# Attention and two MoE layers on one core: K and Q of the second pair loaded earlier, a third V buffer, block sums copied by DMA, a shorter warm-up

## The chip, the core and the metric

The kernel runs on one core of one Trainium2 chip. The time is that of one execution on the device in microseconds (us), and the median over three runs is what counts. The engines of the core are TensorE (PE; its weight loads are shown apart as PEld), VectorE (DVE), ScalarE (ACT), GpSimd (POOL) and SyncE (SP), whose queue issues most of the DMAs. Each engine takes its own list of instructions in order and waits on semaphores.

## What is computed

```
block, window = 32, 16            # q, k, v: (2, 8, 768, 64); nb = 24 blocks
k_sum = max of k over each block; v_sum = mean of v over each block
s_l = scale * q k^T, kept only where |i - j| < window
s_s = scale * q k_sum^T + log(block)
a = softmax over [s_l, s_s];  x = a @ [v, v_sum]
u = x + (relu(x^T w_tok1) w_tok2)^T         # tokens
y = u + relu(u w_ch1) w_ch2                 # channels, 1536 wide
out = y + relu(norm(y) * g w2_ch1) w2_ch2   # channels, 2048 wide
```

## The kernel before

**Attention.** Two heads make a pair; there are eight pairs. A pair has three quads of four windows of 64 queries, so 24 quads run in all. A window of 64 queries sees 96 keys and 24 block entries, so every score row has 120 columns. For a quad n the steps are: `att_qk` (PE, tile `scores`), `att_exp` (the mask step on DVE into `sn` with its minimum `mn`, then the exponential on ACT into `pr`), `att_tr` (PE transposes into `pt`), `att_evac` (copy of `pt` to `PT`, on DVE for every third quad, else on ACT), `att_av` (PE, `av`), `att_norm` (DVE: reciprocal `rec`, product into `u`), `att_hi` (ACT: `xh`) and `att_lo` (POOL: `xl`).

**Preparation of a pair i.** `load_pair` loads K and Q, `load_vt` the transposed V, `load_v` the two halves of V (rows for even and odd windows). `prep_k` takes block maxima of K on DVE (`ks`), and `copy_k` writes them in seven copies into K on ACT. `prep_v1` sums VT over blocks: for pair 0 in one DVE reduction, for the others in four halving steps and two last sums on POOL, into `Z`. `prep_v2` transposes `Z` on PE (`psv`) and copies the result, scaled by 1/32, into 24 rows of V for each of six windows: four ACT instructions for two halves and two heads. So V's rows are 96 rows of values, 24 of block sums, and one guard row that a DMA fills once. Column 64 of the block rows is one; it was set by a memset. K, Q have three buffers, V, VT and Z two.

**Weights.** `load_half` loads 512 KB of weights into a `stage` buffer (three of them). A tick of `conversion` takes the absolute value on ACT (`dec`, L114), four DVE operations (L128 to L136), a rounded copy on ACT (`wh`, L176) and the rest on DVE (`wl`, L183). In attention two such operations go with each `att_norm`. The MoE matmuls (`g1`, `g2`, then `g3`, `g4`) use the high and low parts. Parts of `g1` and `g2` are woven into attention.

**Order.** `ORDER` gives each step a position in units of a quad; `attention` sorts all steps by position and emits them. A builder then makes a fixed list for every engine from that, in which an instruction whose inputs it takes to come late can stand behind later ones: in the trace POOL's list has `xl` of quad 0 (position 6.25) ahead of the sums of pair 1 (position 0.3). The list does not change at run time. The score tile has two slots in shared banks, so the scores of a quad wait for the mask step of the quad before.

**Start.** The first loads stand in `run`: K(0), mask, ident, VT(0), V(0), guard rows, K(1), Q(1), g, VT(1), V(1), all on SP; only Q(0) is on ACT's queue. 24 warm-up matmuls, in blocks of six fp32r and bf16 ones by turns, stand ahead of the first scores in PE's list.

Of the kernel before, what the change touches and what calls it, by code (L numbers as in the profile page):

```python
# [10 lines left out]
F32 = mybir.dt.float32  # L11
F32R = mybir.dt.float32r
U32 = mybir.dt.uint32
AF = mybir.ActivationFunctionType
# [4 lines left out]
P = 128  # L19
B, H, S, D = 2, 8, 768, 64  # L20
BLOCK, WINDOW = 32, 16
NB = S // BLOCK
# [4 lines left out]
NK = 96 + NB  # L27
VC = 136
# [3 lines left out]
LEAD = 3  # L32
NXN = 3
ORDER = {
    "load_k": -5.2, "load_vt": -6.45, "load_v": -0.2, "kmax": -1.75, "copy_k": -0.45, "vsum": -2.7,
    "vput": -0.15, "vput0": 1.35, "kmax1": -2.05, "copy1": -1.35, "vsum0": -3.0, "exp": 1.0, "tr": 2.1,
    "evac": 3.15, "av": 3.65, "norm": 4.55, "hi": 4.85, "lo": 6.25, "late": 22.53, "conv": 4.0, "ops": 2,
    "bg": 9, "bgd": 1.04, "bgt": 0.05, "fin": 0.16,
# [11 lines left out]
def f32(ap):  # L50
    return ap.bitcast(F32)


class Kern:
# [161 lines left out]
    def load_v(self, i):  # L216
        nc = self.nc
        b, p = divmod(i, NPAIR)
        V = self.V[i % 2]
        nc.sync.dma_start(V[NB:NK, 0], self.v[b, p, 0])  # L220
        nc.sync.dma_start(V[0:96, 1], self.v[b, p, 1])

# [34 lines left out]

    def prep_v2(self, i):
        nc = self.nc
        V, Z = self.V[i % 2], self.Z[i % 2]  # L260
        ps = self.ps_pt.tile([P, 512], F32, tag="pt", name=f"psv{i}")
        nc.tensor.transpose(ps[:NK, 0:P], Z, self.ident)  # L262
        for a, j in ((0, 0), (96, 1)):
            for r in range(2):
                nc.scalar.activation(  # L265
                    V[a : a + NB, j, :, 65 * r : 65 * r + 64],
                    ps[a : a + NB, r * 64 : r * 64 + 64]
                    .rearrange("p (o n) -> p o n", o=1)
                    .to_broadcast([NB, 6, 64]),
                    AF.Copy,  # L270
                    scale=1.0 / BLOCK,
                )

    def att_qk(self, n):
        nc = self.nc
# [58 lines left out]
    def att_av(self, n):  # L334
        nc = self.nc
        i, qd = divmod(n, 3)
        V = self.V[i % 2]
        pt = self.pt.pop(n)
        ps = self.ps_av.tile([P, 2, 132], F32, tag="av", name=f"av{n}")
        self.av[n] = ps  # L340
        for e in range(2):
            for r in range(2):
                for j in range(2):
                    u = 2 * e + j
                    nc.tensor.matmul(  # L345
                        ps[64 * j : 64 * j + 64, e, 65 * r : 65 * r + 65],
                        pt[:, u * P + 64 * (r ^ j) : u * P + 64 * (r ^ j) + 64],
                        V[:, j, 2 * qd + e, 64 * r : 64 * r + 65],
                        start=True,
                        stop=True,  # L350
                    )
# [264 lines left out]
    def run(self):  # L616
        tc, nc, ctx = self.tc, self.nc, self.ctx
# [26 lines left out]
        att = self.att  # L644
        self.Q = [att.tile([P, S], F32, name=f"Q{i}") for i in range(3)]
        self.K = [att.tile([P, 7, 184], F32, name=f"K{i}") for i in range(3)]
        self.PT = [att.tile([NK + 1, 512], F32, name=f"PT{i}") for i in range(2)]
        self.V = [att.tile([NK + 1, 2, 6, VC], F32, name=f"V{i}") for i in range(2)]
        self.VT = [att.tile([P, S], F32, name=f"VT{i}") for i in range(2)]
        self.Z = [att.tile([P, NK], F32, name=f"Z{i}") for i in range(2)]  # L650
        self.u = const.tile([P, B * ST, C], F32, name="u")
# [5 lines left out]
        self.hh = [xp.tile([P, 2, C], F32R, name=f"hh{i}") for i in range(B)]  # L657
        self.hl = [xp.tile([P, 2, C], F32R, name=f"hl{i}") for i in range(B)]

        warm = [att.tile([P, 512], dt, name=f"warm{i}") for i, dt in enumerate((F32R, mybir.dt.bfloat16))]  # L660
        nc.vector.memset(f32(warm[0]), 0.0)
        nc.gpsimd.memset(warm[1], 0.0)
        for t in self.Z:
            nc.gpsimd.memset(t, 0.0)
        for t in self.V:
            nc.gpsimd.memset(t[0:NB, 0, :, 64:65], 1.0)
            nc.gpsimd.memset(t[96:NK, 1, :, 64:65], 1.0)
        for t in self.PT:
            nc.vector.memset(t[96 : NK + 1], 1.0)
        self.load_pair(0, nc.scalar)  # L670
        nc.sync.dma_start(self.mask, self.mask_in)
        nc.sync.dma_start(self.ident, self.ident_in)
        self.load_vt(0)
        self.load_v(0)
        for t in self.V:
            nc.sync.dma_start(t[NK : NK + 1], self.guard)
        self.load_pair(1)
        nc.sync.dma_start(self.gt, self.g)
        self.load_vt(1)
        self.load_v(1)  # L680

        wps = self.ps_mm.tile([P, 512], F32, tag="mm", name="warm_ps")
        for i in range(24):
            w = warm[i // 6 % 2]
            nc.tensor.matmul(wps, w[:, :P], w, start=True, stop=True)  # L685

        self.attention()
        actx.close()
# [27 lines left out]
        for n in range(len(units) + 1):  # L716
# [3 lines left out]
            if n < len(units):  # L720
                kind, s, f, g = units[n]
                nf = F1 if kind == "u" else F2
                c = 3 + f if kind == "u" else 3 + F1 + f
# [117 lines left out]
```

## Time and profile before

| | |
|---|---|
| median of 3 runs | 604.87 us (603.02 to 605.31) |
| profiled execution, its own time | 604.47 us |
| its span, first to last instruction | 602.7 us |
| mean granted TensorE clock | 0.977 |
| PE, DVE, ACT, POOL busy | 583.0, 339.3, 208.2, 44.2 us |
| DMA | 51.80 MB, mean 86 GB/s |

Busy times are sums over the span. PE's busy time counts the time between a matmul's start and its modelled end, so a busy PE need not be at its peak. The granted clock is given as a share of 2.4 GHz; 0.50 is 1.2 GHz. Attention's last `av` runs at 103 us; what follows is matmul work with the conversion of the remaining weights beside it.

### The profile page before, as it was taken

To read this page: it belongs to the slowest core of one execution; us is meant where nothing else is said; L and a number is where in the kernel's file an instruction comes from. 1 tells how busy PE (TensorE), PEld (TensorE's weight loads), DVE (VectorE), ACT (ScalarE), POOL (GpSimd) and SP (SyncE) were. 2 spreads that over 40 slices of the span, in tenths; PEclk is the share of its full clock that TensorE was granted. 3 is DMA by queue.
4 is the path that set the end of the run, shared out by engine and by line. 5 is a ranking of instruction groups with operands and counts; after the bars stand their busy time and mean duration, and the time that the engine had idled before them with its cause. 6 is when DMAs were issued, how large, how long until landed. Compare 5 with 4: busy or idle time off the path is not lost.

```text
span 602.7 us, 9099 instructions
## 1 busy us (share of the span) xinstructions
PE 583.0 (97%) x3560; PEld 509.3 (85%) x3560; DVE 339.3 (56%) x855; ACT 208.2 (35%) x458; POOL 44.2 (7%) x77
## 2 busy tenths in 40 slices
PE   7777999999999999999999999999999999999997
PEld 4555778789899889998988998999988999989896
DVE  4489988999378899787799931111153211111122
ACT  4678895544233444334354401101022111011110
POOL 0474622000000000000000000000000000000000
PEclk9679899999999999999999999999999999999999
DMA  9977933235224333234323100000010100000011
GB/s 279 309 223 212 281 89 106 71 131 184 71 104 141 104 106 105 80 129 138 107 77 128 42 1 0 1 0 1 1 52 2 52 1 1 0 1 0 1 54 52
DMA packets 21503, 51.80 MB, mean 86 GB/s; under 512 B 2002, under 2 KB 8402, under 8 KB 21460
## 3 DMA queue, kind: packets, MB, share of 16 engines
q1 hardware_dynamic: 21316, 50.83, 25.5%
q8 instruction: 28, 0.46, 0.3%
q10 hardware_dynamic: 144, 0.39, 0.2%
q14 instruction: 15, 0.12, 0.1%
HBM read 48.07 MB, written 3.15 MB: 85 GB/s over the span
## 4 chain that ended last, share of the span: by engine, by line
PE 90%; DVE 3%; ACT 3%; POOL 2%; issue 1%; POOLq 0%; DVEq 0%; ACTq 0%
PE scores L285 2%; PE g L199 2%; PE g L201 2%; PE g L200 2%; PE av L345 1%; PE pt L322 1%; PE warm_ps L685 1%; POOL VT L253 1%; PE tx L506 1%; POOL xl L385 1%; ACT V L265 1%; DVE sn L305 1%; PE acc_('x', 2)_0_4702 L200 1%; PE acc_('x', 0)_0_3701 L200 1%; PE acc_('x', 0)_2_3703 L200 1%
## 5 line engine op out<-in xcount | busy, mean ns | idle before, releaser
L136 DVE SCALAR_TENSOR_TENSOR dec<-stage,dec 128x512 uint32<-128x512 uint32 x62 | 43.5, 702 | 0.8
L183 DVE TENSOR_TENSOR wl<-dec,wh 128x512 fp32r<-128x512 f32 x62 | 43.1, 697 | 1.2 <-ACT wh L176 1.1
L132 DVE SCALAR_TENSOR_TENSOR dec<-stage,dec 128x512 uint32<-128x512 uint32 x62 | 43.1, 696 | 0.9
L176 ACT CAST wh<-dec 128x512 fp32r<-128x512 f32 x62 | 38.0, 616 | 13.8 <-DVE dec L136 13.5
L114 ACT ACTIVATE dec<-stage 128x512 f32<-128x512 f32 x62 | 41.6, 673 | 3.0 <-DMA stage<-in_wts_dram 2.3
L315 ACT ACTIVATE pr<-sn,mn 128x120 f32<-128x120 f32 x96 | 30.9, 384 | 3.9 <-DVE mn L305 3.5
L128 DVE TENSOR_SCALAR dec<-dec 128x512 f32<-128x512 f32 x62 | 27.8, 450 | 1.5 <-ACT dec L114 1.4
L130 DVE TENSOR_SCALAR dec<-dec 128x512 uint32<-128x512 uint32 x62 | 26.5, 428 | 0.8
L305 DVE CUSTOM_DVE_ANT_0 sn<-scores,mask 128x120 f32<-128x120 f32 x96 | 21.6, 277 | 8.6 <-PE scores L285 7.2
L322 PE MATMUL pt<-ident,pr 128*120 128x128 f32 x96 | 21.3, 321 | 3.1 <-ACT pr L315 2.5
L385 POOL TENSOR_TENSOR xl<-u,xh 128x256 fp32r<-128x256 f32 x24 | 19.4, 811 | 59.3 <-ACT xh L376 59.3
L345 PEld LDWEIGHTS av<-V,PT 121*64 121x64 f32 x384 | 15.5, 151 | 9.0 <-issue 4.7
L345 PE MATMUL av<-V,PT 121*64 121x65 f32 x384 | 19.5, 244 | 3.2 <-DVE u L362 1.4
L285 PE MATMUL scores<-K,Q 64*64 64x120 f32 x384 | 18.5, 309 | 3.6 <-ACT K L237 2.0
L322 PEld LDWEIGHTS pt<-ident,pr 128*120 128x120 f32 x96 | 11.9, 150 | 9.0 <-ACT pr L315 5.2
L253 POOL TENSOR_TENSOR VT<-VT 128x384 f32<-128x384 f32 (+3 forms) x28 | 19.3, 690 | 1.6
L285 PEld LDWEIGHTS scores<-K,Q 64*64 64x64 f32 x384 | 11.8, 150 | 8.7 <-DVE mn L305 2.3
L265 ACT ACTIVATE V<-psv 24x384 f32<-24x384 f32 x32 | 14.5, 478 | 7.6 <-PE psv L262 7.2
L199 PE MATMUL g<-xh,wh 128*128 128x256 f32 x48 | 15.1, 322 | 0.0
L200 PE MATMUL g<-xl,wh 128*128 128x256 f32 x48 | 14.3, 303 | 0.5 <-POOL xl L385 0.5
L201 PE MATMUL g<-xh,wl 128*128 128x256 f32 x48 | 14.6, 309 | 0.0
L481 DVE TENSOR_SCALAR xn<-u,mv,rs 128x128 f32<-128x128 f32 x48 | 14.0, 341 | 0.0
(3005 smaller groups left out, 1676.5 us busy)
## 6 DMA issues: line engine op xcount, KB each, us to landing
stage<-in_wts_dram SPq DMA_DIRECT2D x62, 512.0 KB, 3.2
V<-in_v_dram SPq DMA_DIRECT2D x16, 306.0 KB, 5.1
K<-in_k_dram SPq DMA_DIRECT2D x8, 480.0 KB, 5.9
VT<-in_vt_dram SPq DMA_DIRECT2D x8, 384.0 KB, 5.1
out_dram<-u SPq DMA_DIRECT2D x12, 256.0 KB, 2.1
Q<-in_q_dram SPq DMA_DIRECT2D x7, 384.0 KB, 6.3
Q<-in_q_dram ACTq DMA_DIRECT2D x1, 384.0 KB
mask<-in_mask_dram SPq DMA_DIRECT2D x1, 240.0 KB, 4.6
```

What stands on the lines that cost most here:

```text
L114: nc.scalar.activation(m, self.raw[n][:, :, 1].bitcast(F32), AF.Abs)
L128: nc.vector.tensor_scalar(m, m, MAG_LO, MAG_HI, op0=ALU.max, op1=ALU.min)
L132: nc.vector.scalar_tensor_tensor(mi, t[:, :, 1], 0xC0000000, mi, op0=ALU.bitwise_and, op1=ALU.bitwise_or)
L136: nc.vector.scalar_tensor_tensor(mi, t[:, :, 0], 29, mi, op0=ALU.logical_shift_right, op1=ALU.bitwise_or)
L176: self.nc.scalar.copy(self.slots[c if c < 16 else c - 16][0][:, s], x)
L183: self.nc.vector.tensor_tensor(wl[:, s], x, f32(wh[:, s]), op=ALU.subtract)
L200: nc.tensor.matmul(out, lhs[0], rhs[1], start=False, stop=False)
L285: nc.tensor.matmul(ps[cols, j, e, :NK], Q[rows, 64 * w : 64 * w + 64], K.rearrange("p v c -> p (v c)")[rows, a : a + NK], start=True, stop ...
L305: nc.vector.tensor_tensor_reduce(sn[:, u], ps[:, u % 2, u // 2, :NK], self.mask[:, mv], scale=-SCALE, scalar=3e38, op0=ALU.add, op1=ALU.mi ...
L315: nc.scalar.activation(pr[:, u], sn[:, u], AF.Exp, bias=mn[:, u : u + 1], scale=-1.0)
L322: nc.tensor.transpose(ps[:NK, u * P : u * P + P], pr[:, u], self.ident)
L345: nc.tensor.matmul(ps[64 * j : 64 * j + 64, e, 65 * r : 65 * r + 65], pt[:, u * P + 64 * (r ^ j) : u * P + 64 * (r ^ j) + 64], V[:, j, 2 * ...
```

## The change

The first loads get another order: K(1) and Q(1) go ahead of V(0), VT(1) right behind V(0), and the guard rows to ACT's queue. V has three buffers, and `load_v` moves from position -0.2 to -3.2. Pair 0 keeps its four ACT copies. From pair 1 on, `prep_v2` writes the block sums once, by one ACT instruction into a small tile `VS`, and two DMAs on SP's queue copy them from there into the six windows, with the column of ones. The warm-up has 13 bf16 matmuls in place of 24 mixed ones.

```diff
-    "load_v": -0.2,
+    "load_v": -3.2,
 def load_v(self, i):
-        V = self.V[i % 2]
+        V = self.V[i % 3]
 def prep_v2(self, i):
-        V, Z = self.V[i % 2], self.Z[i % 2]
+        V, Z, VS = self.V[i % 3], self.Z[i % 2], self.VS[i % 2]
         ps = self.ps_pt.tile([P, 512], F32, tag="pt", name=f"psv{i}")
         nc.tensor.transpose(ps[:NK, 0:P], Z, self.ident)
+        if i == 0:
...
+            return
+        nc.scalar.activation(
+            VS.rearrange("p (r c) -> p r c", r=2)[:, :, 0:64],
+            ps[:NK, 0:P].rearrange("p (r c) -> p r c", r=2),
+            AF.Copy,
+            scale=1.0 / BLOCK,
+        )
         for a, j in ((0, 0), (96, 1)):
-            for r in range(2):
-                nc.scalar.activation(
-                    V[a : a + NB, j, :, 65 * r : 65 * r + 64],
-                    ps[a : a + NB, r * 64 : r * 64 + 64]
-                    .rearrange("p (o n) -> p o n", o=1)
-                    .to_broadcast([NB, 6, 64]),
-                    AF.Copy,
-                    scale=1.0 / BLOCK,
-                )
+            nc.sync.dma_start(
+                V[a : a + NB, j, :, 0:129],
+                VS[a : a + NB, 0:129].rearrange("p (o n) -> p o n", o=1).to_broadcast([NB, 6, 129]),
+            )
 def run(self):
-        self.V = [att.tile([NK + 1, 2, 6, VC], F32, name=f"V{i}") for i in range(2)]
+        self.V = [att.tile([NK + 1, 2, 6, VC], F32, name=f"V{i}") for i in range(3)]
+        self.VS = [att.tile([NK, 130], F32, name=f"VS{i}") for i in range(2)]
-        warm = [att.tile([P, 512], dt, name=f"warm{i}") for i, dt in enumerate((F32R, mybir.dt.bfloat16))]
-        nc.vector.memset(f32(warm[0]), 0.0)
-        nc.gpsimd.memset(warm[1], 0.0)
+        warm = att.tile([P, 512], mybir.dt.bfloat16, name="warm")
+        nc.vector.memset(warm, 0.0)
-        for t in self.V:
-            nc.gpsimd.memset(t[0:NB, 0, :, 64:65], 1.0)
-            nc.gpsimd.memset(t[96:NK, 1, :, 64:65], 1.0)
+        nc.gpsimd.memset(self.V[0][0:NB, 0, :, 64:65], 1.0)
+        nc.gpsimd.memset(self.V[0][96:NK, 1, :, 64:65], 1.0)
+        for t in self.VS:
+            nc.gpsimd.memset(t[:, 64:65], 1.0)
         self.load_vt(0)
+        self.load_pair(1)
         self.load_v(0)
+        self.load_vt(1)
         for t in self.V:
-            nc.sync.dma_start(t[NK : NK + 1], self.guard)
-        self.load_pair(1)
+            nc.scalar.dma_start(t[NK : NK + 1], self.guard)
         nc.sync.dma_start(self.gt, self.g)
-        self.load_vt(1)
         self.load_v(1)
-        for i in range(24):
-            w = warm[i // 6 % 2]
-            nc.tensor.matmul(wps, w[:, :P], w, start=True, stop=True)
+        for _ in range(13):
+            nc.tensor.matmul(wps, warm[:, :P], warm, start=True, stop=True)
```

## Rows read from the trace of the kernel before

**Rows 1.** Windows: busy us (count) of PE, PEld, DVE, ACT, POOL; granted clock; DMA.

```profile
8.00:16.00 8.00, 5.39 (x75) 3.29 (x75) 3.56 (x26) 5.62 (x17) 0.00 (x0) 0.83 1.06 298
16.00:24.00 8.00, 4.73 (x46) 3.15 (x43) 3.41 (x15) 3.96 (x12) 5.70 (x12) 0.50 0.88 306
24.00:32.00 8.00, 7.71 (x118) 5.69 (x120) 5.48 (x31) 6.83 (x19) 0.97 (x3) 0.82 0.95 296
...
40.00:60.00 20.00, 16.70 (x197) 12.22 (x193) 17.92 (x70) 17.30 (x46) 10.18 (x16) 0.84 0.79 248
...
80.00:100.00 20.00, 20.00 (x262) 15.71 (x261) 18.62 (x77) 14.59 (x42) 5.62 (x8) 1.00 0.27 86
...
120.00:140.00 20.00, 19.38 (x98) 17.14 (x97) 19.46 (x39) 8.98 (x16) 0.00 (x0) 1.00 0.41 139
```

**Rows 2.** Timeline, 0 to 11 us: start, length, engine, operation, count, idle before.

```profile
1.46 8.00 PE L685 MATMUL warm_ps<-warm 128*128 128x512 f32 x24 [1.46 <-DVE warm L661]
...
5.07 0.15 PEld L685 LDWEIGHTS <-warm 128*128 128x128 bf16 x1 [0.28 <-issue]
...
5.49 0.15 PEld L685 LDWEIGHTS <-warm 128*128 128x128 bf16 x1 [0.28 <-issue]
...
6.25 0.33 ACT L237 COPY K<-ks 128x168 f32<-128x168 f32 x1 [3.81 <-DVE ks L227]
...
7.73 0.95 DVE L245 TENSOR_REDUCE Z<-VT 128x24 f32<-128x768 f32 x1 [1.51 <-DMA VT<-in_vt_dram]
...
9.39 0.64 PE L285 MATMUL scores<-K,Q 64*64 64x120 f32 x16
...
10.10 0.28 DVE L305 CUSTOM_DVE_ANT_0 sn<-scores,mask 128x120 f32<-128x120 f32 x1 [1.20 <-PE scores L285]
```

**Rows 3.** Timeline, 15 to 22 us.

```profile
15.18 1.23 PE L345 MATMUL av<-V,PT 121*64 121x65 f32 x16 [1.20 <-issue]
...
17.00 0.94 DVE L227 TENSOR_REDUCE ks<-K 128x24 f32<-128x768 f32 x1
...
17.68 0.72 POOL L385 TENSOR_TENSOR xl<-u,xh 128x256 fp32r<-128x256 f32 x1 [15.65 <-ACT xh L376]
...
18.36 2.47 POOL L253 TENSOR_TENSOR VT<-VT 128x384 f32<-128x384 f32 x4
...
18.37 1.08 PE L285 MATMUL scores<-K,Q 64*64 64x120 f32 x16 [1.96 <-ACT K L237]
...
21.56 0.47 PE L262 MATMUL psv<-ident,Z 128*120 128x128 f32 x1
```

**Rows 4.** DMAs issued at 6.5 to 6.9, 7.6 to 8, 12.6 to 14: KB, us to landing.

```profile
gt<-in_g_dram SPq DMA_DIRECT2D x1, 2.0 KB, 6.0
...
VT<-in_vt_dram SPq DMA_DIRECT2D x1, 384.0 KB, 6.1
...
stage<-in_wts_dram SPq DMA_DIRECT2D x2, 512.0 KB, 10.3
```

**Rows 5.** Timeline, 28 to 44 us.

```profile
28.03 0.33 PE L262 MATMUL psv<-ident,Z 128*120 128x128 f32 x1
...
28.50 0.47 ACT L265 ACTIVATE V<-psv 24x384 f32<-24x384 f32 x1
...
28.88 0.31 ACT L237 COPY K<-ks 128x168 f32<-128x168 f32 x1
...
29.10 1.36 ACT L265 ACTIVATE V<-psv 24x384 f32<-24x384 f32 x3
...
29.23 0.34 PE L345 MATMUL av<-V,PT 121*64 121x65 f32 x4
...
30.79 0.65 ACT L114 ACTIVATE dec<-stage 128x512 f32<-128x512 f32 x1
...
44.03 0.33 PE L345 MATMUL av<-V,PT 121*64 121x65 f32 x2
```

**Rows 6.** Waits of SP's queue, 0 to 100 us: total, times, longest.

```profile
SPq L166 <- DVE dec L136: 56.1, 11, 12.9
```

More of the change, by code (lines that the diff above doesn't have):

```diff
@@ L34 @@
 ORDER = {
-    "load_k": -5.2, "load_vt": -6.45, "load_v": -0.2, "kmax": -1.75, "copy_k": -0.45, "vsum": -2.7,
+    "load_k": -5.2, "load_vt": -6.45, "load_v": -3.2, "kmax": -1.75, "copy_k": -0.45, "vsum": -2.7,
     "vput": -0.15, "vput0": 1.35, "kmax1": -2.05, "copy1": -1.35, "vsum0": -3.0, "exp": 1.0, "tr": 2.1,
@@ L259, in prep_v2 @@
         nc = self.nc
-        V, Z = self.V[i % 2], self.Z[i % 2]
+        V, Z, VS = self.V[i % 3], self.Z[i % 2], self.VS[i % 2]
         ps = self.ps_pt.tile([P, 512], F32, tag="pt", name=f"psv{i}")
         nc.tensor.transpose(ps[:NK, 0:P], Z, self.ident)
-        for a, j in ((0, 0), (96, 1)):
-            for r in range(2):
-                nc.scalar.activation(
-                    V[a : a + NB, j, :, 65 * r : 65 * r + 64],
-                    ps[a : a + NB, r * 64 : r * 64 + 64]
-                    .rearrange("p (o n) -> p o n", o=1)
-                    .to_broadcast([NB, 6, 64]),
-                    AF.Copy,
-                    scale=1.0 / BLOCK,
-                )
+        if i == 0:
+            for a, j in ((0, 0), (96, 1)):
+                for r in range(2):
+                    nc.scalar.activation(
+                        V[a : a + NB, j, :, 65 * r : 65 * r + 64],
+                        ps[a : a + NB, r * 64 : r * 64 + 64]
+                        .rearrange("p (o n) -> p o n", o=1)
+                        .to_broadcast([NB, 6, 64]),
+                        AF.Copy,
+                        scale=1.0 / BLOCK,
+                    )
+            return
+        nc.scalar.activation(
+            VS.rearrange("p (r c) -> p r c", r=2)[:, :, 0:64],
+            ps[:NK, 0:P].rearrange("p (r c) -> p r c", r=2),
+            AF.Copy,
+            scale=1.0 / BLOCK,
+        )
+        for a, j in ((0, 0), (96, 1)):
+            nc.sync.dma_start(
+                V[a : a + NB, j, :, 0:129],
+                VS[a : a + NB, 0:129].rearrange("p (o n) -> p o n", o=1).to_broadcast([NB, 6, 129]),
+            )
     def att_qk(self, n):
@@ L336, in att_av @@
         i, qd = divmod(n, 3)
-        V = self.V[i % 2]
+        V = self.V[i % 3]
         pt = self.pt.pop(n)
```

## The prediction

> **What bounds the kernel now.** I read the windows first, then the timeline of the first 32 us, the DMA landings in it, and last the waits of the SP queue. TensorE (PE) does most of the work, and the windows show where it does not [rows 1]: at 80 to 100 us PE fills its window (20.00 of 20), but in 8 to 16 it is busy 5.39 of 8 and in 16 to 24 only 4.73 of 8, at a granted clock of 0.50, the 1.2 GHz level. Two things follow. Before some 66 us the kernel is a chain of attention steps in which PE waits; after it, PE works through a fixed amount. So a microsecond taken from the chain in front moves everything behind it, if nothing else holds the later stretch. VectorE (DVE) could: 17.92 of 20 us at 40 to 60, 19.46 of 20 at 120 to 140 [rows 1], most of it weight conversion.
>
> In the timeline of the start the reader should follow four clocks. PE does 24 warm-up matmuls from 1.46 to 9.46, and scores(0) starts at 9.39, though its K was complete at 6.25 + 0.33 = 6.58 [rows 2]. Scores(3), the first of pair 1, starts at 18.37, released by the copy of pair 1's key maxima, whose reduction ran only at 17.00 on DVE, in line behind the result of quad 0 [rows 3]. GpSimd (POOL) did xl(0) at 17.68 and then pair 1's value sums from 18.36 on; its xl(0) had waited for ScalarE (ACT), while VT(1), issued in the window that begins at 7.6, landed 6.1 us after, at about 13.7 [rows 3, 4]. The transpose psv(1) starts at 21.56, and PE's list has pt(1) right behind it: nothing of quads 1 and 2 can be finished before. This moment is the one to move.
>
> **Warm-up.** The bf16 weight loads at 5.07 and 5.49 lie 0.42 to 0.43 us apart: 512 columns in 0.43 us is the 1.2 GHz level. With x matmuls of 0.43 and 24 - x at about 0.235, 8.00 us gives x = (8.00 - 5.64) / 0.195 = 12. So the clock rose after some 12 of them, near 6.6 us. Thirteen take 12 x 0.43 + 0.24 = 5.4 us and end at 6.9, after K's 6.58: scores(0) starts 2.5 us earlier. But DVE's list has the sum of VT(0) before the first mask step, and it starts when VT(0) lands, at 7.73, and keeps DVE to 8.7, and with a small copy to about 8.9. If the list stays so, the mask step goes from 10.10 to 8.9 and only 1.2 us is gained; if not, 2.5. That is the bound from both sides. The full clock has ended by the 16 us window in any case; PE idle in between may end it sooner, at 1.08 instead of 0.64 us for a scores step [rows 2, 3], some 0.4 us on two steps, ahead of a point that the DMA sets (below).
>
> **Loads.** Up to VT(0) nothing moves, so it lands at 7.73 [rows 2]. Behind it now come K(1) and Q(1), then V(0), then VT(1). At the 298 GB/s of 8 to 16 us [rows 1], 480 KB take 1.65 us, 384 KB 1.3 and the two halves of V(0), 612 KB, 2.1: K(1) lands near 9.4, Q(1) at 10.7, V(0) at 12.8. VT(1) has the same bytes ahead of it as before: 13.7. V(0) arrives about 3 us later than it did; what covers it is av(0) at 15.18 [rows 3], or 14.0 with the 1.2 us above. Without that cover, with the whole 2.5 us of the warm-up at av(0), it would cost about 0.2. The three guard rows on ACT's queue take two short issues off SP and cost ACT little before 6 us, where it waits. The memsets (one bf16 tile less on POOL, a half-sized one on DVE) lie ahead of 2 us beside the first loads and change no later start.
>
> With K(1) at 9.4 instead of after V(0), its reduction (0.94 us) and copy can stand ahead of quad 0's result in DVE's list, and scores(3) no longer follows 17.00. Likewise V(0) now lands only one transfer, 1.3 us, ahead of VT(1), where K(1) and Q(1) lay between them; a list made in order of arrival puts VT(1)'s sums before xl(0), which needs av(0), the division and a copy first. Then they run from 13.7; from 18.36 to psv(1) the rows have 21.56 - 18.36 = 3.2 us: psv(1) at about 16.9 to 17.0, 4.6 us earlier than 21.56. This is the largest term. The other bound is the case that POOL and DVE keep the old lists: everything follows av(0), 1.2 to 2.5 us earlier.
>
> **Block sums by DMA.** For pairs 1 to 7, four ACT copies of 0.47 to 0.48 us give way to one of 120x128 elements. The nearest ACT row is 0.31 us for 168 elements [rows 5]; I take 0.3. Then come two DMAs of 24 x 6 x 516 bytes on SP, an operation that the trace of before does not show. Bounds for their landing: nothing, if they are hidden, to 10.3 us, as for the stage loads behind a backlog [rows 4]. The row that is nearest in size is gt: 2.0 KB took 6.0 us [rows 4], so a small transfer waits for what was issued before it.
>
> The Trainium skill, "DMA: Bandwidth & Descriptors", section "Queues, rings and completion order", says that each DMA engine takes data descriptors in ring order; by that rule a short DMA on SP's queue cannot overtake, the trace agrees with gt's 6.0 us, and without the rule the forecast would be 0.9 us lower.
>
> In numbers: the stage loads issued between 12.3 and 13.2 land at about 23.4 [rows 4], and V(2), 612 KB, now follows them (third buffer, no wait for av): 2.1 us more, 25.5. Pair 1's sums, issued near 18, land then. Their first reader, av(3), stood at 29.23 [rows 5]; 4.6 earlier is 24.6. So 0.9 us is given back. For later pairs I count nothing: psv(2) at 28.03 lies 16 us ahead of av(6) at 44.03 [rows 5], more than any landing here; the cost without this cover would be the landing itself, 6 us.
>
> ACT's saving is 4 x 0.478 - 0.3 = 1.6 us a pair. For pair 1 I count nothing: pt(1) and its copy on DVE stand between psv(1) and the next av and do not need ACT. For pair 2 the copies from 28.50 to 30.46 lie back to back with other ACT work [rows 5]: up to 1.6. From 32 on DVE is filled, so ACT's time is free: 0. I take half of pair 2's, 0.8. The third V buffer frees SP of its wait for av; this was no path of its own.
>
> **Sum.** 604.47 (the profiled execution: span 602.7 and 1.8 around it) - 4.6 + 0.9 - 0.8 = 600.0. The median of the runs is 0.4 above that execution; I say 600.2, with 598.5 to 602 as the likeliest case's own range (the 0.9 not paid and all of ACT's 1.6 gained gives 598.7 on the runs; no ACT gain and twice the 0.9 gives 602.1).
>
> **Rivals.** (1) Old lists kept on POOL and DVE: -1.2 to -2.5, and -0.8 from ACT: 601.6 to 602.9. For it: a list is fixed before the run, and 13.7 against 17.68 was not used before either. Against: V(0) and K(1) change places. (2) DVE gives it back: the conversions stay tied to the arrival of the stage loads, which land no earlier, and DVE, full at 120 to 140, makes PE wait there by what was won. Of 4.5 us perhaps 1 is left: 603.5 to 604.5. Against: the stage data lay there from 23.4 and conversion began at 30.79 [rows 5], so the lists, not the data, set the start. (3) Slower: the new DMA parks SP. SP takes its list in order; a block-sum DMA waits for POOL, PE and ACT, and the stage loads, K and Q queued behind it wait too. SP already waited 56.1 us in 11 times, at most 12.9, for stage buffers [rows 6]. If it is parked for the 3.2 us that POOL's sums and their hand-over take [rows 3], ahead of a stage load, in pairs 3 to 5, where DVE is filled, three times 3.2 less the 4.5 gives 610. It decides once a load comes later than the conversion that reads it. Against it: the loads are issued two conversion steps ahead, and V's own waits leave the queue. (4) More than forecast: the shorter chain also closes DVE's 2.5 idle us in 24 to 32 [rows 1] and all ACT gains count: 604.9 - 4.6 - 1.6 - 2.5 = 596.
>
> **Chances.** Forecast 0.52, (1) 0.17, (2) 0.15, (3) 0.08, (4) 0.08. A change under 0.5%, 3.0 us, is about what a measurement of this kernel cannot tell from none: faster is below 601.8. 0.48 of the forecast's 0.52, 0.05 of (1), all of (4): 0.61. Within: 0.04, 0.12 and 0.15: 0.31. Slower: 0.08. For 8 in 10 the range goes from 595.5, below (4), to 604.5, which takes in (2) and leaves out (3).
>
> **What would show it.** Scores(0) near 6.9; K(1)'s reduction before quad 0's reciprocal; POOL's first work on VT(1) near 13.7, ahead of xl(0); psv(1) near 17; block sums landing near 25 and av(3) waiting for a DMA; PE full some 4 to 5 us sooner. I am wrong if POOL's list still begins with xl(0), if PE shows new gaps after 100 us, or if SP's longest wait is one for the small tile VS.

## The result and the profile after

The changed kernel takes 611.48 us (median of 4 runs, 609.69 to 612.16); the kernel before takes 605.09 in the same comparison (4 runs, 603.02 to 605.67). The ratio is 1.0109, with an interval of 1.0088 to 1.013: slower by 6.4 us, where the terms of the forecast add up to 4.5 us faster. The profiled execution took 610.98, its span is 609.2, at a mean granted clock of 0.972.

The windows of the changed kernel answer to [rows 1]; the columns are the same.

```profile
8.00:16.00 8.00, 1.77 (x18) 1.02 (x18) 2.62 (x11) 3.21 (x9) 1.22 (x2) 0.57 1.04 287
16.00:24.00 8.00, 6.27 (x58) 3.92 (x58) 2.93 (x18) 3.25 (x10) 4.06 (x11) 0.50 1.06 363
24.00:32.00 8.00, 6.20 (x92) 4.16 (x91) 6.06 (x29) 5.72 (x17) 3.34 (x6) 0.86 1.08 306
40.00:60.00 20.00, 15.77 (x205) 11.86 (x204) 18.14 (x68) 15.15 (x42) 10.91 (x17) 1.00 0.64 190
80.00:100.00 20.00, 19.90 (x236) 15.05 (x229) 18.50 (x78) 13.44 (x39) 7.71 (x12) 0.98 0.58 153
120.00:140.00 20.00, 18.93 (x94) 16.02 (x93) 19.24 (x38) 8.16 (x16) 0.00 (x0) 1.00 0.38 130
```

PE is now almost empty at 8 to 16 us (1.77 of 8, before 5.39). The DMA share at 80 to 100 us says where to look further: 0.58, where it was 0.27. Loads that had been done by 80 us are still coming.

The timeline of the head, against [rows 2, 3]: start, length, engine, operation, count, and the idle time before it with its releaser.

```profile
1.19 5.22 PE L698 MATMUL warm_ps<-warm 128*128 128x512 bf16 x13 [1.19 <-DVE warm L675]
...
7.64 0.95 DVE L245 TENSOR_REDUCE Z<-VT 128x24 f32<-128x768 f32 x1 [1.24 <-DMA VT<-in_vt_dram]
...
8.90 0.30 PE L262 MATMUL psv<-ident,Z 128*120 128x128 f32 x1 [2.49 <-DVE Z L248]
9.12 0.95 DVE L227 TENSOR_REDUCE ks<-K 128x24 f32<-128x768 f32 x1 [0.32 <-DMA K<-in_k_dram]
9.13 1.08 PE L298 MATMUL scores<-K,Q 64*64 64x120 f32 x16
...
14.71 2.46 POOL L253 TENSOR_TENSOR VT<-VT 128x384 f32<-128x384 f32 x4 [13.25 <-DMA VT<-in_vt_dram]
...
17.71 0.47 PE L262 MATMUL psv<-ident,Z 128*120 128x128 f32 x1 [5.57 <-POOL Z L256]
18.11 1.08 PE L298 MATMUL scores<-K,Q 64*64 64x120 f32 x16
18.21 0.28 ACT L275 ACTIVATE VS<-psv 120x128 f32<-120x128 f32 x1 [5.74 <-PE psv L262]
19.05 0.98 SPq L282 DMA_DIRECT2D V<-VS  x1
```

Two places in PE's list are new. The transposes psv(0) and psv(1) now stand ahead of scores(0) and scores(1). PE therefore waits 2.49 us for Z of pair 0 and 5.57 us for Z of pair 1 with score work behind them that was ready: scores(1) starts at 18.11, where the kernel before had it at 11.40. This costs the head 6.7 us, yet not the end: the twelfth quad's scores start at 51.2 (before 51.9). The delay that lasts arises later: the product of quad 12, the thirteenth, starts at 76.7 (before 67.0), the last quad's scores at 100.3 (before 92.4), and its product at 109.7 (before 103.1), which is about the span's 6.5 us.

SP's queue in that later stretch, and the conversion steps of DVE around it:

```profile
61.13 0.61 SPq L209 DMA_DIRECT2D K<-in_k_dram  x1
...
62.52 0.36 SPq L214 DMA_DIRECT2D VT<-in_vt_dram  x1
74.28 0.34 SPq L166 DMA_DIRECT2D stage<-in_wts_dram  x1
74.73 0.36 SPq L220 DMA_DIRECT2D V<-in_v_dram  x1
...
75.69 1.67 SPq L282 DMA_DIRECT2D V<-VS  x2
77.46 0.61 SPq L209 DMA_DIRECT2D K<-in_k_dram  x1
```

```profile
61.58 0.68 DVE L183 TENSOR_TENSOR wl<-dec,wh 128x512 fp32r<-128x512 f32 x1
69.45 0.47 DVE L128 TENSOR_SCALAR dec<-dec 128x512 f32<-128x512 f32 x1
...
72.72 1.08 DVE L136 SCALAR_TENSOR_TENSOR dec<-stage,dec 128x512 uint32<-128x512 uint32 x1
```

The last pair's K is issued at 77.46, 10.8 us later than before (66.69). SP stood from 62.9 on at one stage load, whose buffer came free with the conversion step that ends at 72.72 + 1.08 = 73.80. So this wait took 10.9 us. The list of SP's waits, against [rows 6], shows that it is no longer in total than before:

```profile
SPq L166 <- DVE dec L136: 47.6, 7, 17.5
SPq L282 <- ACT K L237: 9.8, 1, 9.8
```

The longest, 17.5, is not the one above: it begins at 101.4, when attention's loads are out, as the 12.9 of the kernel before begins at 99.5. The 9.8 is the wait for the last pair's `VS`, from 84.0 to 93.9, with a stage load behind it but no K or V.

### The profile page after: what moved, and what is told of

Same layout as the page of the kernel before. It is cut to its first block, busy times and chain, and to the rows that moved or that the text cites. A ratio compares the mean times of both kernels' runs of the same rounds, so it can differ in the third digit from the quotient of the medians.

```text
span 609.2 us, 9089 instructions
## 1 busy us (share of the span) xinstructions
PE 583.6 (96%) x3549; PEld 509.1 (84%) x3549; DVE 340.2 (56%) x855; ACT 198.3 (33%) x437; POOL 42.1 (7%) x76
## 4 chain that ended last, share of the span: by engine, by line
PE 89%; DVE 5%; DMA 3%; ACT 1%; issue 1%; POOL 1%; SPq 0%; POOLq 0%; DVEq 0%; ACTq 0%
PE av L358 2%; PE scores L298 2%; PE pt L335 2%; PE g L200 1%; PE g L199 1%; DMA VT<-in_vt_dram 1%; PE g L201 1%; DMA Q<-in_q_dram 1%; PE tx L519 1%; DMA mask<-in_mask_dram 1%; DVE sn L318 1%; DVE dec L132 1%; PE acc_('x', 0)_0_3685 L200 1%; PE acc_('x', 2)_0_4686 L200 1%; PE acc_('x', 0)_2_3687 L200 1%
## 5 line engine op out<-in xcount | busy, mean ns | idle before, releaser
L136 DVE SCALAR_TENSOR_TENSOR dec<-stage,dec 128x512 uint32<-128x512 uint32 x62 | 45.0, 725 | 0.8
L132 DVE SCALAR_TENSOR_TENSOR dec<-stage,dec 128x512 uint32<-128x512 uint32 x62 | 43.5, 702 | 0.9
L128 DVE TENSOR_SCALAR dec<-dec 128x512 f32<-128x512 f32 x62 | 27.2, 438 | 3.0 <-ACT dec L114 2.8
L335 PE MATMUL pt<-ident,pr 128*120 128x128 f32 x96 | 23.2, 328 | 4.5 <-ACT pr L328 4.2
L298 PE MATMUL scores<-K,Q 64*64 64x120 f32 x384 | 20.8, 321 | 5.6 <-DVE mn L318 5.6
L358 PEld LDWEIGHTS av<-V,PT 121*64 121x64 f32 x384 | 18.5, 167 | 6.4 <-issue 4.1
L358 PE MATMUL av<-V,PT 121*64 121x65 f32 x384 | 22.8, 261 | 0.0
L398 POOL TENSOR_TENSOR xl<-u,xh 128x256 fp32r<-128x256 f32 x24 | 18.1, 759 | 54.6 <-ACT xh L389 54.6
L298 PEld LDWEIGHTS scores<-K,Q 64*64 64x64 f32 x384 | 12.8, 156 | 10.6 <-DVE mn L318 6.9
L335 PEld LDWEIGHTS pt<-ident,pr 128*120 128x120 f32 x96 | 12.1, 151 | 10.9 <-ACT pr L328 7.3
L200 PE MATMUL g<-xl,wh 128*128 128x256 f32 x48 | 13.7, 293 | 0.7 <-POOL xl L398 0.6
L199 PE MATMUL g<-xh,wh 128*128 128x256 f32 x48 | 13.8, 299 | 0.4 <-ACT xh L389 0.4
L201 PE MATMUL g<-xh,wl 128*128 128x256 f32 x48 | 13.7, 290 | 0.0
L345 ACT COPY PT<-pt 120x512 f32<-120x512 f32 x16 | 9.1, 582 | 9.3 <-PE pt L335 4.6
## 6 DMA issues: line engine op xcount, KB each, us to landing
V<-VS SPq DMA_DIRECT2D x14, 72.6 KB
```

The source lines that it names most:

```text
L132: nc.vector.scalar_tensor_tensor(mi, t[:, :, 1], 0xC0000000, mi, op0=ALU.bitwise_and, op1=ALU.bitwise_or)
L136: nc.vector.scalar_tensor_tensor(mi, t[:, :, 0], 29, mi, op0=ALU.logical_shift_right, op1=ALU.bitwise_or)
L200: nc.tensor.matmul(out, lhs[0], rhs[1], start=False, stop=False)
L298: nc.tensor.matmul(ps[cols, j, e, :NK], Q[rows, 64 * w : 64 * w + 64], K.rearrange("p v c -> p (v c)")[rows, a : a + NK], start=True, stop ...
L335: nc.tensor.transpose(ps[:NK, u * P : u * P + P], pr[:, u], self.ident)
L358: nc.tensor.matmul(ps[64 * j : 64 * j + 64, e, 65 * r : 65 * r + 65], pt[:, u * P + 64 * (r ^ j) : u * P + 64 * (r ^ j) + 64], V[:, j, 2 * ...
```

## The experiments

Each kernel is the kernel before with the edit shown, unless another is named. Ratios are to the kernel before on the same chip, with their intervals.

**Which part carries the loss.** Four kernels: the block sums alone, the loads alone, the warm-up alone, and the changed kernel with the ACT copies back.

```diff
 sums_only:   block sums by VS and two transfers on SP, as in the change; loads, warm-up, two V buffers as before
 loads_only:  first loads in the changed order, guards on ACT's queue; nothing else
 warm_only:   13 bf16 warm-up matmuls; nothing else
 no_sums:     changed kernel, with the four ACT copies per pair
```

> The kernel before with the block sums by DMA alone (two V buffers, old load order, old warm-up). Theory Q (SP's queue: a block-sum DMA stands behind stage loads and in front of K, Q and stage loads, and the last pairs come late by it): most of the change's 6.4 us, 609 to 612. Theory H (the head: the new load order puts psv(1) ahead of scores(1) in PE's list, and that delay reaches the end): no loss here, 603 to 606.

> The kernel before with the new order of the first loads alone (guard rows on ACT's queue included). Theory H: PE's list has psv(0) ahead of scores(0) and psv(1) ahead of pt(1), quads 1 and 2 late by some 6 us, 608 to 612. Theory Q: the head's delay is absorbed before quad 12, 603 to 606.

> The kernel before with the 13 bf16 warm-up matmuls alone. Both theories: scores(0) near 7 instead of 9.4 and psv(1) still held by POOL's list; 602 to 605. Slower than 606 would speak for a third theory, that the earlier fall of the granted clock costs more than the 2.5 us.

> The changed kernel with the four ACT copies back in place of the block-sum DMAs for all pairs (new load order, third V buffer and short warm-up stay). Theory Q: the loss is gone, 600 to 605. Theory H: it stays, 609 to 612.

| kernel | median us | ratio (interval) |
|---|---|---|
| sums_only | 610.34 | 1.0091 (1.006 to 1.0122) |
| loads_only | 604.11 | 0.9983 (0.9951 to 1.0015) |
| warm_only | 604.97 | 0.9996 (0.9977 to 1.0014) |
| no_sums | 605.54 | 1.0016 (0.9996 to 1.0037) |

The block sums carry the whole loss; loads and warm-up move the end by nothing that can be measured. In no_sums scores(1) starts as late (19.6) as in the changed kernel, so the slip at the head is absorbed. In warm_only scores(0) starts at 6.9, and that gain is absorbed too.

**SP, the landing, or PE's list.** Three readings: Q, SP's queue is held; W, the first product of a pair waits for the landing; L, PE's list puts that product behind the next quad's transposes.

```diff
 dummy_sums:  ACT copies stay; VS and the two transfers go to a tile that nobody reads
-                V[a : a + NB, j, :, 0:129],
+                self.VD[a : a + NB, j, :, 0:129],
 sums_actq:   sums_only, issued on ACT's queue
-            nc.sync.dma_start(
+            nc.scalar.dma_start(
 list_only:   ACT copies; av(3i) behind the transposes of quad 3i+2
+            with self.tc.issue_after(self.last_tr.ins):
+                self.att_av_mm(n)
 sums_pinned: sums_only; the transposes of quad 3i+2 behind av(3i)
+            with self.tc.issue_after(self.last_av.ins):
+                self.att_tr_mm(n)
```

> The kernel before with its ACT copies of the block sums kept; beside them the VS activation and the two transfers per pair are issued on SP's queue too, but into a tile that nobody reads. Theory Q (SP's queue is held: two issues of 0.8 us per pair stand behind stage loads and ahead of the next K, Q and stage loads, and each parks the queue until psv is there): the loss stays, 609 to 611. Theory W (the first attention product of a pair waits for the landing): nobody waits, so 605 to 606, the 7 extra activations of 0.3 us being all that is added. Theory L (the build lists the first product of a pair behind the next quad's transposes, and the two PT buffers and the scores back up): the list stays nearly that of the kernel before, 605 to 606.

> Block sums by transfer alone on the kernel before (as in the run of 610.3), the two transfers issued on ACT's queue right behind the VS activation that they need. Theory Q: SP is as before, so 604 to 606 (ACT loses 2 issues per pair in place of the 4 copies). Theory W: the landing comes some 2 to 5 us sooner since nothing parks ahead of it, but is still waited for: 605 to 608. Theory L: the list still has the first product of a pair behind the next quad's transposes in most pairs: 607 to 611.

> The kernel before with its ACT copies, SP untouched; only PE's list is changed, so that the first product of each pair from the second on stands behind the transposes of the pair's last quad, as it stands with the block sums by transfer. Theory Q: 604 to 606. Theory W: 604 to 606. Theory L: 608 to 611, psv and scores late from the third pair on as with the transfers.

> Block sums by transfer on SP's queue, and PE's list pinned the other way: the transposes of a pair's last quad stand behind the pair's first product, as in the kernel before. Theory Q: 609 to 612, SP's list being the same. Theory W: 610 to 614, PE now stands still until each landing. Theory L: 604 to 606.

Measured: dummy_sums 610.84 (1.0114, 1.0075 to 1.0152), sums_actq 609.12 (1.009, 1.0056 to 1.0123), list_only 605.63 (1.0022, 1.0009 to 1.0036), sums_pinned 615.44 (1.0173, 1.0139 to 1.0206). With nobody waiting for the sums the loss is all there, so W falls as the main cause. PE's list moved by this one quad costs 1.3 us, and pinned back it costs 5 us more than sums_only, above all three forecasts: L falls as I had put it, for PE's list alone. Two results don't fit my theories. In dummy_sums I had expected PE's list to stay nearly that of the kernel before; it did not, and it moved further than in list_only (below). And sums_actq, where Q said 604 to 606, came out in L's range. SP's waits in its trace (us in total, times, longest):

```profile
SPq L166 <- DVE dec L136: 32.6, 6, 13.9
SPq L209 <- DMA V<-VS: 16.3, 4, 6.7
SPq L220 <- PE psv L262: 11.9, 2, 10.6
SPq L221 <- DMA V<-VS: 8.0, 1, 8.0
SPq L166 <- DMA V<-VS: 4.1, 1, 4.1
```

As the profile puts the waits down, SP's K, V and stage loads wait 28.4 us for block-sum transfers that another queue issues. K(5) goes out at 48.5 (before 40.9), though it reads and writes nothing of theirs. In this trace the transfers on ACT's queue signal seven of the eight semaphores that SP's loads signal too; in sums_poolq below they signal eight others. Another queue did not set SP free.

**GpSimd's queue, and the stage loads off SP.**

```diff
 sums_poolq, after_poolq: sums_only and the changed kernel, issued on GpSimd's queue
-            nc.sync.dma_start(
+            nc.gpsimd.dma_start(
 sums_stagepool, before_stagepool: sums_only and the kernel before, weight stage loads on GpSimd's queue
-            self.nc.sync.dma_start(t.rearrange("p n t -> p (n t)"), ...)
+            self.nc.gpsimd.dma_start(t.rearrange("p n t -> p (n t)"), ...)
```

> Block sums by transfer alone on the kernel before, the two transfers of a pair issued on GpSimd's queue. In the run on ACT's queue, SP's K and V loads were seen to wait for a block-sum transfer that another queue issues (28.4 us in 6 waits). Theory Q2 (what costs is SP's next loads being tied to the block sums, by the queue's order or by sharing the eight semaphores that its transfers go round): GpSimd's transfers are counted apart, so SP runs as before: 603 to 606. Theory W2 (the landing itself, or the 72 KB in small pieces, costs): 608 to 611 as on the other queues. GpSimd's issue of the two transfers is not in any trace so far; should it take more than some 2 us per pair, the xl subtractions behind it come late and the time lies between.

> The changed kernel with the two block-sum transfers of a pair on GpSimd's queue. Theory Q2: with SP free of them the changed kernel comes to that of the run with the ACT copies back (605.5) or below it by what the copies cost ACT: 602 to 605.5. Theory W2: 608 to 612.

> Block sums by transfer on SP's queue on the kernel before, but the weight stage loads (SP stood 32 to 56 us of the attention on their buffers) issued on GpSimd's queue. Theory Q2, if the order behind the stage loads is what makes the sums late: 603 to 606 where the run below (the same move without the block sums) is at 604 to 606; if the sums hold V, K and Q among themselves: some 3 to 5 us above the run below. Theory W2: 5 us above the run below.

> The control for the run above: the kernel before with its ACT copies, and only the weight stage loads on GpSimd's queue. Both theories: no forecast beyond 600 to 609, since GpSimd's own waits for the conversions now hold its xl subtractions and VT sums; it is the base from which the run above is read.

Measured: sums_poolq 607.09 (1.0055, 1.0036 to 1.0074), after_poolq 607.01 (1.0049, 1.0029 to 1.0069), sums_stagepool 615.33 (1.0185, 1.0162 to 1.0208), before_stagepool 611.18 (1.0107, 1.0071 to 1.0144). On GpSimd's queue half the loss is left, for the changed kernel less than half (2.5 of 6.4 us): between the two theories for both. POOL's groups and waits in sums_poolq show what this queue pays instead:

```profile
L282 POOL DMA_DIRECT2D V<-VS x14 | 8.6, 617 | 9.0 <-ACT K L237 3.8 <-ACT pr L328 3.8 <-ACT VS L275 1.4
```

The 14 issues keep POOL for 8.6 us, and it stands another 9.0 us in front of them; pair 2's sums of V queue behind, and psv(2) starts at 30.0 (before 28.0). The pair with the stage loads on GpSimd settles little: POOL is then the engine that is parked, both are slow, and the block sums still cost 4.2 us on top.

**Is it the late conversion.** In the versions with the full transfers and the stage loads both on SP, DVE's order has the conversion later: ahead of the twelfth quad's mask steps stand 19 of its steps (those of L128 to L136) in the kernel before and in list_only, sums_actq and sums_poolq, but 12 in sums_only, dummy_sums and sums_pinned, and 15 in the changed kernel.

```diff
 late_dec:    ACT copies; conversion steps put off
+        put(11.5, lambda: setattr(self, "ops", 0))
+        put(15.5, lambda: setattr(self, "ops", 2))
 sums_ops3, before_ops3: sums_only and the kernel before
-    "conv": 4.0, "ops": 2,
+    "conv": 4.0, "ops": 3,
 loads_pin2:  loads_only; psv(0) behind scores(0), psv(1) behind scores(2)
+            with self.tc.issue_after(self.pin[i].ins):
+                nc.tensor.transpose(ps[:NK, 0:P], Z, self.ident)
```

> The kernel before with its ACT copies and SP's queue free of block sums; only the weight conversion is put off: none of its steps goes with the quads' results for four quads, so that DVE has 17 of them ahead of the thirteenth to fourteenth quads' mask steps where the kernel before has 20 to 23, and 18 against 25 ahead of the fifteenth: 5 to 8 late, as with the block sums on SP. Theory D (the loss is the late conversion: stage buffers come free late, SP's later loads stand behind them): 608 to 611. Theory H (SP held by the block-sum transfers themselves): 603 to 606.

> Block sums by transfer on SP's queue with the conversion drawn forward, three steps in place of two with each quad's result: 16 steps ahead of the eleventh quad's mask steps and 24 ahead of the fourteenth, as many as the kernel before or more. Theory D: within 2 us of the control with the ACT copies and the same three steps. Theory H: 4 to 6 us above that control.

> The control: the kernel before with its ACT copies, three conversion steps in place of two with each quad's result. Neither theory says where it lies; 601 to 609, and it is the base of the run above.

> The first loads in the changed order on the kernel before (604.1 as the build lists it, the second block-sum transpose ahead of the second quad's scores), with PE's list pinned so that the first block-sum transpose stands behind the first quad's scores and the second behind the third quad's. If PE's list ate the gain of the head: 600 to 602, as forecast. If the slack between the head and the stretch where DVE is busy without a gap (48 to 64 us) eats it whatever PE does: 603.5 to 605.5.

Measured: late_dec 605.74 (1.0016, 0.9998 to 1.0035), sums_ops3 610.03 (1.0113, 1.0077 to 1.0148), before_ops3 606.32 (1.0028, 1.0008 to 1.0048), loads_pin2 604.39 (1.0002, 0.998 to 1.0024; 12 runs from 601.88 to 608.32). Late conversion by itself costs next to nothing, and drawn forward it does not heal the transfers: 3.7 us above the control. That is neither within theory D's 2 us nor quite in theory H's 4 to 6, but theory D as stated falls. (Three steps a quad did not bring the conversion level with the control: 18 steps against 22 ahead of the twelfth quad. They did bring it level with the kernel before, which has 19, 20 and 23 steps ahead of the twelfth to fourteenth quads where sums_ops3 has 18, 21 and 24, and the loss is still whole.) The profiled execution of loads_pin2 has a span of 600.5, 2.2 below that of the kernel before, but the runs as a whole show no gain.

**The wait or the transfer.** The last two split dummy_sums.

```diff
 dummy_free:  the two transfers read a constant tile; the VS activation is gone, SP waits for nothing
 dummy_wait:  VS stays and SP waits for it; one small transfer in place of the two
-        for a, j in ((0, 0), (96, 1)):
-            nc.sync.dma_start(self.VD[a : a + NB, j, :, 0:129], ...)
+        nc.sync.dma_start(self.VD[0:NB, 0, 0, 0:129], VS[0:NB, 0:129])
```

> As the run in which nobody reads the transferred sums (610.8): the kernel before with its ACT copies, and the two transfers of a pair on SP's queue into a tile that nobody reads; here they read a constant tile, so that SP waits for no activation, and the VS activation is gone. Theory P (SP parks on VS): 604 to 606. Theory T (the transfers themselves, 0.8 us of issue each, and the order that the build makes around them): 609 to 611.

> The other half: the VS activation is kept and SP waits for it at the same place of its queue, but the transfer behind it is a single one of 24 rows of 516 B in place of two of 144 rows each, into a tile that nobody reads. Theory P: 609 to 611. Theory T: 604 to 606.

Measured: dummy_free 612.81 (1.0141, 1.0108 to 1.0174), dummy_wait 605.06 (1.0006, 0.999 to 1.0021). Theory P falls on both sides. Transfers that wait for nothing and that nobody reads cost the full loss, and more than theory T's 609 to 611; a queue that stands 10.8 us in six waits, up to 2.4 at a time, for the VS activation, with the loads behind it, costs nothing. (Number and size of the transfers change together here: one of 12.1 KB in place of two of 72.6 KB. Which of the two matters is not shown.) SP's queue and the conversion steps just ahead, first dummy_free:

```profile
72.74 0.88 DVE L136 SCALAR_TENSOR_TENSOR dec<-stage,dec 128x512 uint32<-128x512 uint32 x1
```

```profile
62.37 0.38 SPq L214 DMA_DIRECT2D VT<-in_vt_dram  x1
73.68 0.33 SPq L166 DMA_DIRECT2D stage<-in_wts_dram  x1
74.13 0.35 SPq L220 DMA_DIRECT2D V<-in_v_dram  x1
...
75.39 1.68 SPq L277 DMA_DIRECT2D VD<-VS  x2
77.18 0.61 SPq L209 DMA_DIRECT2D K<-in_k_dram  x1
```

Then dummy_wait:

```profile
64.40 0.94 DVE L136 SCALAR_TENSOR_TENSOR dec<-stage,dec 128x512 uint32<-128x512 uint32 x1
```

```profile
61.02 0.38 SPq L214 DMA_DIRECT2D VT<-in_vt_dram  x1
65.42 0.33 SPq L166 DMA_DIRECT2D stage<-in_wts_dram  x1
65.85 0.37 SPq L220 DMA_DIRECT2D V<-in_v_dram  x1
...
68.15 0.83 SPq L282 DMA_DIRECT2D VD<-VS  x1
69.09 0.58 SPq L209 DMA_DIRECT2D K<-in_k_dram  x1
```

And late_dec, where conversion is late too:

```profile
63.79 0.33 SPq L220 DMA_DIRECT2D V<-in_v_dram  x1
...
65.65 0.55 SPq L209 DMA_DIRECT2D K<-in_k_dram  x1
...
68.91 0.35 SPq L166 DMA_DIRECT2D stage<-in_wts_dram  x1
```

The same queue is shown three times. In the first two the stage load goes out 0.06 and 0.08 us after the conversion step that frees its buffer; V and K of the last pairs are listed behind it and go out within 4 us. When the step ends at 73.6, V and K go at 74 and 77; when it ends at 65.3, at 66 and 69; and in late_dec, where the stage load stands behind V and K in SP's list, they go at 64 and 66 although conversion is late. The traces of the versions whose stage loads stay on SP divide the same way:

| kernel | stage load ahead of K(7) us | K(7) issued us | later quads transposed ahead of quad 12's product | span us | ratio of the runs |
|---|---|---|---|---|---|
| loads_pin2 | 60.8 | 64.3 | 1 | 600.5 | 1.0002 |
| late_dec | 54.5 (the next, 68.9, behind it) | 65.7 | 1 | 604.3 | 1.0016 |
| loads_only | 63.7 | 66.0 | 1 | 602.7 | 0.9983 |
| before | 64.4 | 66.7 | 1 | 602.7 | 1 |
| warm_only | 66.2 | 67.6 | 1 | 604.0 | 0.9996 |
| after_poolq | 65.5 | 67.8 | 1 | 604.9 | 1.0049 |
| list_only | 66.6 | 68.0 | 2 | 604.4 | 1.0022 |
| before_ops3 | 64.7 | 68.9 | 1 | 604.3 | 1.0028 |
| dummy_wait | 65.4 | 69.1 | 1 | 603.3 | 1.0006 |
| sums_poolq | 67.2 | 69.0 | 1 | 604.5 | 1.0055 |
| sums_actq | 65.0 | 69.0 | 1 | 605.8 | 1.009 |
| no_sums | 64.8 | 69.2 | 1 | 606.0 | 1.0016 |
| sums_ops3 | 70.6 | 75.2 | 3 | 607.0 | 1.0113 |
| sums_only | 72.6 | 76.0 | 3 | 608.1 | 1.0091 |
| dummy_sums | 72.6 | 76.1 | 3 | 607.7 | 1.0114 |
| dummy_free | 73.7 | 77.2 | 3 | 608.0 | 1.0141 |
| changed kernel | 74.3 | 77.5 | 3 | 609.2 | 1.0109 |
| sums_pinned | 75.6 | 79.0 | 1 (pinned) | 614.2 | 1.0173 |

No span up to 606.0 has K(7) after 69.2, and none from 607.0 on has it before 75.2. But a span is that of the one profiled execution: in sums_actq it is among the shortest of eight, and by the runs that kernel loses as much as sums_only with K(7) at 69.0. So the late K(7) goes with the loss where the transfers stand on SP's queue. The loss on ACT's queue, and the half on GpSimd's, are not told by it.

The late K(7) is also not where the delay begins. Quad 12's product (the first of pair 4) needs V(4), which is issued at 56.1 in dummy_free and at 54.6 in dummy_wait. PE's transposes and products, first in dummy_free (quads 13, 14, 15 transposed, then the products of 12 and 13):

```profile
66.52 0.60 PE L330 MATMUL pt<-ident,pr 128*120 128x128 f32 x4
68.51 0.65 PE L330 MATMUL pt<-ident,pr 128*120 128x128 f32 x4
69.92 0.27 PE L330 MATMUL pt<-ident,pr 128*120 128x128 f32 x1
71.32 0.54 PE L330 MATMUL pt<-ident,pr 128*120 128x128 f32 x3
72.72 0.45 PE L353 MATMUL av<-V,PT 121*64 121x65 f32 x4
```

then in dummy_wait (quad 13 transposed, then the product of 12), as in the kernel before:

```profile
67.03 0.54 PE L332 MATMUL pt<-ident,pr 128*120 128x128 f32 x3
67.50 0.33 PE L355 MATMUL av<-V,PT 121*64 121x65 f32 x2
```

In dummy_free the product is 5.2 us later than in dummy_wait, at 72.7, and K(7) goes out only at 77.2. When K(7) has landed (at 82.0, 4.8 us after its issue), it lies there until DVE reduces it:

```profile
91.58 0.94 DVE L227 TENSOR_REDUCE ks<-K 128x24 f32<-128x768 f32 x1
```

So the lists of PE and DVE, which the build makes anew around the transfers, are a rival to SP's queue that stands. The table's fourth column divides the versions on SP's queue as K(7) does, but for sums_pinned. There PE's order was put back by hand and the loss grew, so PE's list alone is not it. A run with the full transfers and all lists of the kernel before is missing.

## Why the prediction was wrong

The forecast added -4.6 for psv(1), +0.9 for av(3) and -0.8 for ACT. (The sum's 600.0 and the 0.4 between that execution and the median give 600.4, not 600.2; the 598.7 and 602.1 of the range start from 600.4.) The clocks of the head came largely as forecast; what they were worth at the end, and what the transfers do to later pairs, did not.

- **Warm-up.** Thirteen matmuls took 5.22 us (5.4 forecast) and ended at 6.41; alone they bring scores(0) to 6.9, as forecast. In the changed kernel psv(0) stands ahead of scores(0) and takes that gain away (9.13). I watched DVE's list there and not PE's.
- **Loads.** K(1)'s reduction runs at 9.12, ahead of quad 0's result (K(1) forecast for 9.4). POOL's first work on VT(1) starts at 14.71, ahead of xl(0) (13.7 forecast). psv(1) starts at 17.71: 3.85 earlier where 4.6 was forecast. What is short is VT(1)'s landing (14.7; the forecast's own landing of V(0), 12.8, and its 1.3 us for VT(1) would have given 14.1). So the mechanism was right. Not forecast was that PE's list puts psv(1) ahead of scores(1), so that PE waits 5.57 us for it.
- **The step from psv(1) to the end failed.** The largest term was passed on in full, "if nothing else holds the later stretch". loads_only has psv(1) at 18.3 and is worth nothing (0.9983, 0.9951 to 1.0015). In its trace the lead is 3.2 us at psv(1) but 0.1 at psv(2) and, after a loss of 1.0 at psv(3), 1.7 at psv(4), 0.5 at psv(5) and 0.1 at psv(6). With PE's list pinned (loads_pin2) it is 2.8 at psv(3), so PE's list takes a part at the head; in loads_only the rest is gone in the stretch where DVE has no gap left (8.00 of 8 us at 56 to 64). That is rival (2) in its outcome (chance 0.15); its reason, the arrival of the stage loads, was not tested. Pinned, the profiled execution keeps 2.0 us at psv(7) and the runs show nothing, so whether the last 2 us can be had stays open.
- **The step that the later pairs cost nothing failed, and with it the sign.** It was argued from the distance of psv(2) to av(6), 16 us, as though only the reader of the sums could wait. sums_only is 610.34, and dummy_free shows that no reader is needed. What is late is the products, clearly from pair 4 on (quad 12's by 8.0 us in sums_only, by 9.7 in the changed kernel), and after them SP's queue, behind one stage load: V(5) by 8.6 us and K(7) by 9.3 in sums_only, K(7) by 10.8 in the changed kernel. The VS activation itself was sized well (0.28 us, 0.3 forecast). The issues were not sized at all: 1.67 us of SP for a pair's two.
- **The landing in front of the reader**, the +0.9 of the sum, is there and is small. What PE waited for in front of its products over the whole attention (us, times) has the line

```profile
  DMA V<-VS: 0.3, 1
```

  so what was forecast for the landing was too much, and the cost lay elsewhere. The product itself, av(3), starts at 34.4, where 25.5 was forecast and the kernel before has 29.2: PE's list has it behind the transposes of quads 4 and 5.
  The ring order that the Trainium skill gives (DMA: Bandwidth & Descriptors, section "Queues, rings and completion order") stood behind the 0.9. The same section says that a later transfer may complete before an earlier one, so the rule is one of the order of starting, and the forecast's "cannot overtake" says more than it. The profile gives no landing for these transfers on SP's queue, so no run here tells whether it holds for them.
- **Rival (3)**, at 0.08, has the sign and the size (610). Its mechanism, SP parked on VS ahead of the loads, is refuted as the cause by the last two runs: dummy_free has the loss without such a wait, dummy_wait has 10.8 us of such waits without a loss. SP's longest wait is for a conversion (17.5; 10.9 within attention), not for VS (9.8), so the sign that I had named for this case did not show either. The rival's other sentence, that "it decides once a load comes later than the conversion that reads it", points at the right queue from the wrong end: in these traces the conversion comes late and holds the load.
- **ACT's saving** (-0.8 forecast). ACT's busy time fell from 208.2 to 198.3 us; with SP free of the transfers (after_poolq) the kernel is still not faster than before, though there POOL pays for the issues. No run shows any of it at the end.

Shown: the loss comes from the two full-size transfers of a pair, without a reader and without a wait; on SP's queue it goes with late products from pair 4 on and with the late K(7). Not shown is the way from the one to the other. Read from the traces alone: PE's, DVE's and SP's lists change with the transfers, and the stage load that stands ahead of V and K goes out late. Late conversion by itself does not do it (late_dec), nor does PE's list by itself (list_only, sums_pinned), and in sums_ops3 the loss is there with the conversion level with the kernel before. No run had the full-size transfers with all lists held in their old order. So how much of the loss is the new order, and how much the transfers' own time on the queue, stays open. (The one stage load behind such a backlog whose landing sums_only gives, issued at 46.1, took 7.2 us; the one at 47.5 before took 4.1.) It stays open too why the transfers cost 4.2 us with the stage loads on GpSimd, where K(7) goes out only 1.0 us later.

## What to carry to other kernels

When work moves from an engine to a DMA on a shared in-order queue, list what stands behind it there and what frees the buffers those loads wait for; the distance to the reader of the moved data says little. Where a build orders the engines itself, a new transfer reorders all of them: compare the order of every engine's list (here products and weight conversion) and of each queue before trusting a sum of durations. A gain at the head may be gone before the end, as here ahead of the stretch where DVE is full, and a run of that part alone tells this cheaply.

## What the hardware showed that I had not expected

- Issuing cost follows the kind of transfer more than its bytes: a 72.6 KB block-sum transfer of 516-byte pieces keeps SP for about 0.8 us, and so does the single 12.1 KB one of dummy_wait (0.83), while a 306 KB half of V takes 0.33 to 0.38. On GpSimd the same issue takes 0.62 us (14 in 8.6).
- Three guard rows on ACT's queue held it from 1.14 to 5.67, but not by their issue: two were out by 2.20, the third went out at 5.45 after a wait for the semaphore that it shares with K(0). ACT's table load stood behind it until 5.71 (in loads_only, with two rows, 2.19), and the first copy of key maxima came at 7.00 where it had come at 6.25 [rows 2].
- By the profile, K and stage loads on SP waited 20.4 us in five waits for transfers issued on ACT's queue with which they share no tile, but semaphores (sums_actq).
